# The second MLP's output products by seven products of quarters for eight, and squares of queries and keys loaded directly into SBUF

## The chip, the cores and the metric

The kernel runs on one core of one Trainium2 chip. The metric is the device time of one execution in microseconds (us). Engines are named as the profile names them: PE is the tensor engine (PEld its weight loads), DVE the vector engine, ACT the scalar engine, POOL the GpSimd engine, SP the engine that issues most DMAs.

## The reference

```python
scores = q @ k.T / sqrt(64)          # 4 batches, 8 heads, 576 positions, head size 64
scores = where(0 <= i - j < 64, scores, -1e9)
attn   = softmax(scores) @ v         # -> x, 2304 tokens x 512
x = (silu(x @ wg1) * (x @ wv1)) @ wo1          # first MLP, 512 -> 1536 -> 512
return (sigmoid(x @ wg2) * (x @ wv2)) @ wo2    # second MLP, the same sizes
```

Queries, keys and values are float32, the weights float64; the output is float32.

## The kernel before

Matrix products are done to nearly full float32 precision with three products of rounded operands: every operand is split into a high part (a copy on ACT) and a low part (a subtraction on DVE), and `TERMS` multiplies high by high, low by high and high by low. So one product of blocks is three matmul steps, and every operand costs one ACT and one DVE instruction more.

**Attention and first MLP** run interleaved. Tokens lie in five tiles of 512 or 384; the loop over tiles and twelve blocks of d_ff counts a number g up by three for each block: the gate product, the value product (`product`, L441), and the output product of the block before (`out_product`, L452). Work for later tiles hangs in tables `before`, `during` and `after`, keyed by g, and is issued on the engines' queues when the loop comes to that g. `plan_attention` places the attention of one 128-token block i there. For the blocks from `TURN` (8) on, queries and keys are turned by DVE transposes of 32x32 squares (`turn`, L231); for that they must lie in SBUF as squares. `to_squares` (L131) copies them into that form from DRAM to DRAM, and `load_qk` (L143) loads the result.

**Weights of the second MLP** are prepared meanwhile. The inputs are rounded from 64 bits (`round_a`, `round_b`: L384 to L399, two ACT and three DVE instructions for a tile of 128x512). For the gate and value weights `operands` makes the sums of quarters that a seven-product scheme needs (`sums`), splits them (`upper`, `lower`: L611, L616) into tiles called `stage`, and stores these in DRAM by POOL (`away`, L624). Stage tiles and raw weights share a ring of four buffers (`raw_p`). The output weights are only rounded, and stored whole (`store`, L406).

**The second MLP** takes three pairs of 384-token halves. In each, six units of d_ff run `strassen` twice (gate, then value): seven products instead of eight, each six matmul steps 384 wide (L775), with sums on DVE behind them (L761), and the product gate times value (L765). Then `outs` does the output products plainly: for each of twelve blocks of d_ff, six output tiles of 128 tokens by 512, three steps each (L840). Beside it DVE and ACT split the hidden values (`split_hidden`), load and split the output weights (`wo2_load`, `wo2_split`: L423, L427), and make the next pair's operands (`x_steps`: L95, L96, L704). Six banks of PSUM hold the sums until the end of the stage, where they are copied out (L860, L862) and stored (L864).

Each engine works its queue in order. A buffer of a pool is given again only when its last reader is done, and the DMA or instruction that wants it waits at the head of its queue.

Of the kernel before, what the change touches and what calls it, by code (L numbers as in the profile page):

```python
# [37 lines left out]
def attention_moe_moe(  # L38
# [86 lines left out]
    squares = {nm: dram.tile([128, HP, NT // 32, 32], FP32, name=f"{nm}s") for nm in "qk"}  # L125

    def to_squares(nm, b, s, hp, par):
        src = {"q": q, "k": k}[nm][b, 2 * hp + par, s:S]
        for a in range(2):
            r0 = 64 * par + 32 * a  # L130
            nc.sync.dma_start(  # L131
                out=squares[nm][r0:r0 + 32, hp, (b * S + s) // 32:(b + 1) * S // 32, :],
                in_=src[:, 32 * a:32 * a + 32].rearrange("(t r) d -> r t d", r=32),
            )

    def load_qk(i, pool=None):
        if i < TURN:
            nat[i, "q"] = load_tokens(q, "q", 128 * i, pool)
            nat[i, "k"] = load_tokens(k, "k", 128 * i, pool)
            return  # L140
        for nm, n in (("q", 4), ("k", 6)):
            t = nat_p.tile([128, HP, n, 32], FP32, tag=nm, name=nm)
            nc.sync.dma_start(out=t, in_=squares[nm][:, :, 4 * i + 4 - n:4 * i + 4, :])  # L143
            nat[i, nm] = t
# [210 lines left out]
    def rows(key):  # L355
# [4 lines left out]
        if wide:  # L360
            src = src.bitcast(INT32)
        if nm == "o":
            return src[fc * 128:(fc + 1) * 128, :]
# [3 lines left out]
    def load_raw(key):  # L367
        r = raw_p.tile([128, 1024 if wide else 512], INT32 if wide else FP32, tag="raw", name="raw")
        dst = r if key[1] == "o" else r.rearrange("p (c f) -> p c f", c=CC)
        nc.sync.dma_start(out=dst, in_=rows(key))  # L370
        raws[key] = r
# [31 lines left out]

    def store(key):
        kept[key] = dram.tile([128, 512], FP32, name=f"k{key[0]}{key[1]}{key[2]}")
        nc.gpsimd.dma_start(out=kept[key], in_=mids.pop(key))  # L406
# [55 lines left out]
    def finish(acc, t, n):  # L462
        for e in range(CC):
# [29 lines left out]
    def plan_attention(i, base, t, col):  # L493
# [8 lines left out]
        if base >= 2:  # L502
            at(during, base - (5 if i < TURN else 6), load_qk, i)
# [26 lines left out]
    for b in range(B):  # L530
        s = max(0, 128 * TURN - W - b * S)
        if s >= S:
            continue
        parts = [(nm, b, s, hp, par) for hp in range(HP) for par in range(2) for nm in "kq"]
        first, last = {1: (10, 24), 2: (25, 41), 3: (46, 77)}[b]
        for j, part in enumerate(parts):
            at(during, first + j * (last - first) // (len(parts) - 1), to_squares, *part)
# [45 lines left out]
    wd = {}  # L583

    def operands(u, j, nm, following):
# [34 lines left out]
        def away(k):  # L620
            if nm == "g":
                n = len(GROUPS[k])
                wd[j, k] = dram.tile([128, 2, n, 2, 256], FP32, name=f"wd{j}_{k}")
            nc.gpsimd.dma_start(out=wd[j, k][:, "gv".index(nm)], in_=stages[k][0].bitcast(FP32))  # L624
# [6 lines left out]
        at(during, u, lower, 0)  # L631
        at(during, u, round_b, keys[1])
        at(during, u, sums, 1)
        at(during, u + 1, away, 0)
# [3 lines left out]
        at(during, u + 2, lower, 1)  # L638
        at(during, u + 2, sums, 3)
        at(during, u + 3, away, 1)  # L640
        at(during, u + 3, lower, 2)
        at(during, u + 4, away, 2)
        at(during, u + 5, upper, 3)
        at(during, u + 6, lower, 3)
        at(during, u + 7, away, 3)
        if following:
            nm_, j_ = following
            at(during, u + 1, load_raw, (1, nm_, 2 * j_))
            at(during, u + 3, load_raw, (1, nm_, 2 * j_ + 1))

    for fc, g in enumerate((39, 41, 43, 46, 48, 50, 52, 57, 59, 61, 66, 68)):
        key = (1, "o", fc)
        at(during, g - 7, load_raw, key)
        at(during, g - 1, round_a, key)
        at(during, g, round_b, key)
        at(during, g + 1, store, key)
    starts = [73, 82, 91, 100, 108, 116, 124, 132, 140, 148, 156, 164]
    groups = [(nm, j) for j in range(JJ) for nm in "gv"]
    at(during, starts[0] - 9, load_raw, (1, "g", 0))
    at(during, starts[0] - 6, load_raw, (1, "g", 1))  # L660
# [154 lines left out]
    def split_hidden(fc):  # L815
        t = []
        for k in range(2):
            t.append(w_p.tile([128, 2, N2], FP32R, tag="g", name="hs"))
            split(t[k][:, 0], t[k][:, 1], hidden[fc][:, k])
        hs[fc] = t  # L820
        hidden.pop(fc)

    def wo2_load(fc):
        t = t_p.tile([128, 512], FP32, tag="t", name="tw")
        nc.sync.dma_start(out=t, in_=kept[1, "o", fc])
        mids[1, "o", fc] = t

    def wo2_split(fc):
        split_hi((1, "o", fc))
        split_lo((1, "o", fc))  # L830

    def outs(p):

        steps = x_steps(p + 1) if p + 1 < PAIRS else []
        acc = [next_bank() for _ in range(6)]
        for fc in range(FC):
            h, w = hs.pop(fc), wts.pop((1, "o", fc))
            for e in range(6):
                for n, (a, b) in enumerate(TERMS):
                    nc.tensor.matmul(  # L840
                        out=acc[e],
                        lhsT=h[e // 3][:, a, e % 3 * 128:(e % 3 + 1) * 128],
                        rhs=w[:, b],
                        start=(fc == 0 and n == 0),
                        stop=(fc == FC - 1 and n == 2),
                    )
            if fc + 2 < FC:
                split_hidden(fc + 2)
                wo2_split(fc + 2)
            if fc + 3 < FC:  # L850
                wo2_load(fc + 3)
            run_steps(steps[0:2] if fc else steps[0:1])
            steps = steps[2:] if fc else steps[1:]
            if fc >= FC - 4:
                w_ahead((p + 1) * JJ * 7 + 3 * (fc - FC + 5))
        assert not steps
        for e in range(6):
            o = t_p.tile([128, 512], FP32, tag="t", name="o")
            if e % 2:
                nc.vector.tensor_copy(o, acc[e])  # L860
            else:
                nc.scalar.activation(out=o, in_=acc[e], func=ACTF.Copy)  # L862
            r0 = p * 2 * N2 + e * 128
            nc.sync.dma_start(out=out[r0:r0 + 128, :], in_=o)  # L864
# [21 lines left out]
    with tc.manual_schedule():  # L886
# [93 lines left out]
        for p in range(PAIRS):  # L980
            for j in range(JJ):
                s = gates()
                beside = []
                if p == 0 and j == 0:
# [9 lines left out]
                    beside = [first, last_outs, lambda: run_steps(steps0[-1:])]  # L994
                strassen(p, j, 0, s, beside)
                if j == JJ - 1:
                    for fc in range(3):
                        wo2_load(fc)
                    for fc in range(2):
# [37 lines left out]
```

## Time and profile before

| | us |
|---|---|
| median of three runs (951.26 to 952.54) | 951.34 |
| the profiled execution | 953.93 |
| its span from first to last instruction | 952.2 |
| PE busy | 937.4 |
| DVE busy | 620.4 |
| ACT busy | 455.2 |

The profiled execution is 2.6 us above the median. Its span ends 1.7 us short of its own time. From 39 us to 541 us the first MLP runs, then the second in three pairs. The three output stages lie at 626.3, 762.7 and 899.1 us and are 49.0 us long each.

### The profile page before, as it was taken

The numbers are of one execution on the slowest core, as the hardware profiler recorded it, in microseconds if no ns is written. First come the engines' busy times: TensorE is split into PE (matmuls) and PEld (weight loads), VectorE is DVE, ScalarE is ACT, GpSimd is POOL, SyncE is SP. The second block draws the span as 40 slices with busy tenths as digits, with TensorE's granted clock in tenths as the row PEclk, the third lists the DMA queues.
The fourth block names the chain that finished last, engine by engine and source line by source line (L and its number), as shares of the span: only waits on it lengthen the run. The fifth ranks groups of instructions, "written<-read, shape, count | busy, mean of one in ns | idle before, by whom it ended". The sixth has DMA issues, their size and how long they took to land.

```text
span 952.2 us, 15825 instructions
## 1 busy us (share of the span) xinstructions
PE 937.4 (98%) x5699; PEld 840.1 (88%) x5699; DVE 620.4 (65%) x1407; ACT 455.2 (48%) x1010; POOL 84.6 (9%) x155
## 2 busy tenths in 40 slices
PE   7899999999999999999999999999999999999998
PEld 6688889899888888888999999988999988999986
DVE  6999985656665565654656566686466684665842
ACT  6898886655565446536344412154221443212332
POOL 3401012100200002100311000000000000000000
PEclk9999999999999999999999999999999999999999
DMA  9679887999976657755799376625868427866411
GB/s 225 190 239 277 269 244 210 307 280 287 285 232 190 198 169 258 221 193 184 242 332 387 137 267 222 246 67 182 268 252 283 152 85 229 290 233 237 139 34 66
DMA packets 183133, 209.70 MB, mean 220 GB/s; under 512 B 89488, under 2 KB 127376, under 8 KB 183056
## 3 DMA queue, kind: packets, MB, share of 16 engines
q1 hardware_dynamic: 171536, 169.38, 57.2%
q0 software_dynamic: 9792, 33.04, 9.5%
q10 hardware_dynamic: 1728, 6.29, 1.7%
q8 instruction: 45, 0.74, 0.3%
q14 instruction: 32, 0.26, 0.1%
HBM read 167.77 MB, written 46.40 MB: 225 GB/s over the span
## 4 chain that ended last, share of the span: by engine, by line
PE 93%; DMA 2%; DVE 2%; ACT 1%; issue 1%; POOL 0%; SPq 0%; DVEq 0%; ACTq 0%
PE g L441 15%; PE v L441 15%; PE a L452 15%; PE a L775 14%; PE att L775 7%; PE a L840 7%; PE att L840 3%; PE v L775 3%; PE g L775 3%; PE g L840 3%; PE v L840 3%; PE att L329 2%; PE att L249 1%; PE att L313 1%; DMA wd<-stage 1%; DVE z L268 1%
## 5 line engine op out<-in xcount | busy, mean ns | idle before, releaser
L452 PE MATMUL a<-h,wo 128*128 128x512 f32 (+1 forms) x720 | 161.4, 372 | 0.3 <-ACT z L286 0.3
L441 PE MATMUL v<-x,wv 128*128 128x512 f32 (+1 forms) x720 | 160.0, 370 | 0.0
L441 PE MATMUL g<-x,wg 128*128 128x512 f32 (+1 forms) x720 | 159.4, 370 | 0.4 <-ACT x L339 0.3
L441 PEld LDWEIGHTS g<-x,wg 128*128 128x128 f32 x720 | 130.7, 188 | 18.4 <-ACT x L339 0.6
L452 PEld LDWEIGHTS a<-h,wo 128*128 128x128 f32 x720 | 129.4, 188 | 19.3 <-issue 2.1
L441 PEld LDWEIGHTS v<-x,wv 128*128 128x128 f32 x720 | 129.9, 188 | 16.6
L775 PE MATMUL a<-xs,wop 128*128 128x384 f32 x756 | 136.2, 334 | 0.0
L775 PEld LDWEIGHTS a<-xs,wop 128*128 128x128 f32 x756 | 131.5, 188 | 0.1
L966 DVE TENSOR_TENSOR s<-s,v 128x512 f32<-128x512 f32 (+1 forms) x60 | 37.9, 632 | 80.8 <-PE v L441 69.7
L767 ACT ACTIVATE s<-s 128x384 f32<-128x384 f32 x72 | 37.9, 526 | 82.2 <-DVE s L761 82.0
L775 PE MATMUL att<-xs,wop 128*128 128x384 f32 x384 | 71.7, 334 | 0.0
L840 PE MATMUL a<-wo,hs 128*128 128x512 f32 x288 | 71.2, 389 | 0.0
L968 ACT ACTIVATE h<-s 128x512 fp32r<-128x512 f32 (+1 forms) x60 | 35.2, 586 | 75.2 <-DVE s L966 75.1
L775 PEld LDWEIGHTS att<-xs,wop 128*128 128x128 f32 x384 | 67.1, 188 | 0.1
L959 ACT ACTIVATE s<-g 128x512 f32<-128x512 f32 (+1 forms) x60 | 33.2, 553 | 67.6 <-PE g L441 66.9
L840 PEld LDWEIGHTS a<-wo,hs 128*128 128x128 f32 x288 | 54.0, 188 | 11.1
L286 ACT ACTIVATE z<-z,nm 128x128 f32<-128x128 f32 x144 | 55.8, 389 | 1.1 <-DVE nm L268 0.9
L397 DVE TENSOR_SCALAR raw<-raw 128x512 uint16<-128x512 uint16 x72 | 55.1, 765 | 1.9 <-ACT raw L384 1.9
L399 DVE CUSTOM_DVE_ANT_0 t<-raw,t 128x1024 uint16<-128x1024 uint16 x72 | 50.2, 697 | 2.5
L384 ACT ACTIVATE raw<-raw 128x512 int32<-128x512 uint32 x72 | 48.4, 672 | 6.2 <-DMA raw<-in_moe_w_out_dram 3.0
L761 DVE TENSOR_TENSOR s<-s,a 128x384 f32<-128x384 f32 x65 | 35.1, 553 | 22.6 <-PE a L775 22.1
L423 ACT ACTIVATE wo<-tw 128x512 fp32r<-128x512 f32 x36 | 22.6, 627 | 54.1 <-PE a L840 26.0
(141 smaller groups left out, 1341.1 us busy)
## 6 DMA issues: line engine op xcount, KB each, us to landing
wop<-wd SPq DMA_DIRECT2D x126, 512.0 KB, 6.0
wo<-k0o SPq DMA_DIRECT2D x48, 512.0 KB, 4.8
wd<-stage POOLq DMA_DIRECT2D x36, 512.0 KB, 5.0
raw<-in_moe_w_gate_dram SPq DMA_DIRECT2D x24, 512.0 KB, 4.7
raw<-in_moe_w_val_dram SPq DMA_DIRECT2D x24, 512.0 KB, 5.4
raw<-in_moe_w_out_dram SPq DMA_DIRECT2D x24, 512.0 KB, 5.7
tw<-k1o SPq DMA_DIRECT2D x36, 256.0 KB, 3.1
k0o<-wo ACTq DMA_DIRECT2D x12, 512.0 KB, 4.9
```

The costliest lines, as they stand in the source:

```text
L286: nc.scalar.activation(out=z[:, hp, :], in_=z[:, hp, :], func=ACTF.Exp, scale=-1.0, bias=nm[:, hp:hp + 1], accum_out=su[:, hp:hp + 1],)
L384: nc.scalar.activation(out=lower, in_=lower.bitcast(UINT32), func=ACTF.Copy, scale=2.0 ** -29)
L397: nc.vector.tensor_scalar(second, fourth, 0x8000, None, ALU.bitwise_and)
L399: nc.vector.tensor_tensor(out=t, in0=t, in1=lower, op=ALU.add)
L441: nc.tensor.matmul(out=ps[:, 0:n], lhsT=w[:, a, c, :], rhs=xt[:, b, c, 0:n], start=(j == 0), stop=(j == len(mm) - 1),)
L452: nc.tensor.matmul(out=acc[e][:, 0:n], lhsT=w[:, a, e * 128:(e + 1) * 128], rhs=h[:, b, 0:n], start=(fc == 0 and j == 0), stop=(fc == FC - ...
L761: nc.vector.tensor_tensor(out=to[out], in0=to[a], in1=ps, op=ALU.add)
L767: nc.scalar.activation(out=to[which], in_=to[which], func=ACTF.Sigmoid)
L775: nc.tensor.matmul(out=ps, lhsT=w[:, val, a, c, :], rhs=xops[op, b][:, c], start=(n == 0), stop=(n == len(mm) - 1),)
L840: nc.tensor.matmul(out=acc[e], lhsT=h[e // 3][:, a, e % 3 * 128:(e % 3 + 1) * 128], rhs=w[:, b], start=(fc == 0 and n == 0), stop=(fc == F ...
L966: nc.vector.tensor_tensor(out=s, in0=s, in1=vps[:, 0:n], op=ALU.mult)
L968: nc.scalar.activation(out=h[:, 0, 0:n], in_=s, func=ACTF.Copy)
```

## The change

Output products: the hidden values and the output weights are cut in quarters (two halves of d_ff units, two halves of tokens or columns), and seven products of sums of quarters take the place of eight, with matmul steps 256 wide. `operands` now prepares the output weights too (six more groups, and closer `starts`), `away` is issued earlier, and `outs` is new. For queries and keys the copies through DRAM go away: `load_squares` loads pieces into SBUF directly, queries by SP and keys by POOL. `turn` transposes only the block's own 128 keys; the 64 before are copied by POOL. Half of the stores of the first MLP's output move from POOL to ACT.

```diff
-    def to_squares(nm, b, s, hp, par):
...
+    def load_squares(i, nm, c, par):
+        if (i, nm) not in nat:
+            nat[i, nm] = nat_p.tile([128, HP, 4, 32], FP32, tag=nm, name=nm)
+        src, eng = {"q": (q, nc.sync), "k": (k, nc.gpsimd)}[nm]
+        for off, m, b, s in runs(128 * i, 128):
+            for a in range(2):
+                r0 = 64 * par + 32 * a
+                eng.dma_start(
+                    out=nat[i, nm][r0:r0 + 32, c, off // 32:(off + m) // 32],
+                    in_=src[b, 2 * c + par, s:s + m, 32 * a:32 * a + 32].rearrange("(t r) d -> r t d", r=32),
...
-        nc.vector.transpose(t, src)
+            nc.gpsimd.tensor_copy(t[:, :, 0:W], st[i - 1, "kt"][:, :, 128:])
+        nc.vector.transpose(t[:, :, -128:], src)
...
-                nc.gpsimd.dma_start(out=x1d[j][:, e, at_:at_ + step], in_=o[:, done:done + step])
+                (nc.gpsimd if e % 2 else nc.scalar).dma_start(out=x1d[j][:, e, at_:at_ + step], in_=o[:, done:done + step])
...
+                at(during, base - 9 + j * 6 // (4 * HP), load_squares, i, "kq"[j % 2], j // 4, j // 2 % 2)
...
-    starts = [73, 82, 91, 100, 108, 116, 124, 132, 140, 148, 156, 164]
+    starts = [39, 48, 58, 66, 75, 81, 87, 93, 100, 107, 114, 120, 126, 132, 138, 145, 155, 161]
+    groups = [("o", j) for j in range(JJ)] + [(nm, j) for j in range(JJ) for nm in "gv"]
...
+    OUT = (1, 2, 6, 7, 5, 4, 3)
+    def h_parts(op, j):
+        (e0, e1), (o0, o1) = [[hidden[2 * j + i][:, n] for n in range(2)] for i in range(2)]
+        if op == 6:
+            y = t_p.tile([128, 512], FP32, tag="t", name="y")[:, 0:N2]
+            h_minus(y, o1, e0)
+            split(*hop(op, j), y)
+            h_minus(o0, o0, y)
+        else:
+            split(*hop(op, j), {1: e0, 2: o0, 7: e1, 5: e0, 4: o0, 3: o1}[op])
...
+    def w2_ahead(upto):
...
+            nc.sync.dma_start(out=t.bitcast(FP32), in_=wdo[k][:, j:j + 2, GROUPS[k].index(op)])
...
+        for k, op in enumerate(OUT):
+            acc = [next_bank()[:, 0:256] for _ in range(3)]
+            for j in range(JJ):
+                i = (7 * p + k) * 3 + j // 2
+                h, w = hops.pop((op, j)), w2s[i][:, j % 2]
+                for e in range(3):
+                    for n, (a, b) in enumerate(TERMS):
+                        nc.tensor.matmul(out=acc[e], lhsT=h[a][:, e * 128:(e + 1) * 128], rhs=w[:, b],
...
+                if j % 2:
+                    w2s.pop(i)
+                    w2_ahead(min(i + 6, (p + 1) * 21))
+                for _ in range(2 if k == 0 and j % 3 == 1 else 1):
+                    if parts:
+                        h_parts(*parts.pop(0))
+                if k >= 2 and (k * JJ + j) % 2 == 0:
+                    run_steps(steps[0:1])
...
+            for e in range(3):
+                if op == 1:
+                    nc.scalar.activation(out=room(0)[e], in_=acc[e], func=ACTF.Copy)
+                elif op == 2:
+                    add(1, 0, acc, e)
+                    leave(1, e)
...
+                if j:
+                    beside = [lambda j=j, n=n: h_early(j - 1, n) for n in range(3)]
```

The first quarters of five of the six units (`h_early`) are made during the units before the stage. What `add` and `leave` issue are additions from PSUM on DVE and stores of 128x256.

The first output stage on PE, before (`a_...`, `g`, `v` are PSUM banks, `hs` the split hidden values, `wo` the split weights):

```order
L840 MATMUL a_6781<-wo,hs 128x512 x3
L840 MATMUL a_6782<-wo,hs 128x512 x3
L840 MATMUL a_6783<-wo,hs 128x512 x3
L840 MATMUL a_6784<-wo,hs 128x512 x3
L840 MATMUL g<-wo,hs 128x512 x3
L840 MATMUL v<-wo,hs 128x512 x3
```

and now, where the first unit of d_ff of the first and of the second of the seven products stand (`w_...` are the loaded sums of weights):

```order
L895 MATMUL a_7162<-w_7074,hs 128x256 x3
L895 MATMUL a_7163<-w_7074,hs 128x256 x3
L895 MATMUL a_7164<-w_7074,hs 128x256 x3
...
L895 MATMUL a_7254<-w_7080,hs 128x256 x3
L895 MATMUL g<-w_7080,hs 128x256 x3
L895 MATMUL v<-w_7080,hs 128x256 x3
```

Six banks for the whole stage became three banks for each of seven products, and the steps are half as wide.

On DVE the last stage's work before was a repeated pair, splits of hidden values (L96) and of weights (L427), behind the last product gate times value (L765):

```order
L761 TENSOR_TENSOR hid<-hid,a_9342 128x384
L765 TENSOR_TENSOR hid<-hid,s 128x384
L96 TENSOR_TENSOR hs<-hid,hs 128x384 x2
L427 TENSOR_TENSOR wo<-tw,wo 128x512
L96 TENSOR_TENSOR hs<-hid,hs 128x384 x2
```

Now, at the start of the first output stage (L757 is the product gate times value, L824 a difference of hidden quarters, `y` a scratch tile):

```order
L757 TENSOR_TENSOR hid<-hid,s 128x384
L96 TENSOR_TENSOR hs<-hid,hs 128x384
L824 TENSOR_TENSOR hid<-hid 128x384 x2
L96 TENSOR_TENSOR hs<-hid,hs 128x384 x6
L824 TENSOR_TENSOR y<-hid 128x384
L96 TENSOR_TENSOR hs<-y,hs 128x384
L824 TENSOR_TENSOR hid<-hid,y 128x384
...
L96 TENSOR_TENSOR hs<-hid,hs 128x384 x2
L878 TENSOR_TENSOR o<-o,a_7254 128x256
L878 TENSOR_TENSOR o<-o,g 128x256
L878 TENSOR_TENSOR o<-o,v 128x256
```

The group of three with `y` stands six times, and all of it stands ahead of the additions (L878) that free the second product's banks.

On POOL, in the third tile, the stores of stage tiles stood alone before:

```order
L624 DMA wd_0_3139<-stage 128x1024
L624 DMA wd_1_3203<-stage 128x1024
L624 DMA wd_2_3240<-stage 128x1024
L624 DMA wd_3_3344<-stage 128x512
```

and now there are loads of key squares (L136) between them:

```order
L622 DMA wdo_2055<-stage 128x1024
L226 COPY kt<-kt 128x4x64
L622 DMA wdo_2128<-stage 128x1024
L136 DMA k<-in_k_dram 32x2x32 x8
L622 DMA wdo_2156<-stage 128x1024
L136 DMA k<-in_k_dram 32x2x32 x16
L622 DMA wdo_2270<-stage 128x512
```

This is the block with the most pieces, 32; the other nine have 16.

## Rows read from the trace of the kernel before

**Rows 1.** The page's head: span, then busy time and instructions of each engine.

```profile
span 952.2 us, 15825 instructions
PE 937.4 (98%) x5699; PEld 840.1 (88%) x5699; DVE 620.4 (65%) x1407; ACT 455.2 (48%) x1010; POOL 84.6 (9%) x155
```

**Rows 2.** Busy time by window: first MLP, two output stages, seven-product units.

```profile
core 0: us, PE busy (x) PEld busy (x) DVE busy (x) ACT busy (x) POOL busy (x), PEclk, DMA share, GB/s
356.00:462.00 106.00, 106.00 (x613) 86.79 (x612) 60.90 (x142) 56.31 (x125) 15.18 (x26) 1.00 0.66 220
626.30:675.30 49.00, 49.00 (x218) 40.58 (x217) 31.67 (x61) 19.98 (x42) 0.00 (x0) 1.00 0.51 163
...
899.10:948.10 49.00, 49.00 (x217) 40.37 (x216) 20.77 (x39) 13.99 (x28) 0.00 (x0) 1.00 0.09 29
840.00:890.00 50.00, 50.00 (x290) 50.00 (x290) 32.62 (x64) 10.06 (x20) 0.00 (x0) 1.00 0.73 256
```

**Rows 3.** Chain that ended last: start us, us, engine, tile, line, count.

```profile
471.82 7.61 DMA wd<-stage
480.59 2.38 PE g L441 x12
...
543.29 4.16 PE a L775 x24
...
626.49 2.76 PE a L840 x12
630.61 2.72 PE a L840 x12
```

**Rows 4.** PE, then its weight loads, in order of time; brackets: idle before.

```profile
98.18 0.60 PE L313 MATMUL att<-ident,z 128*128 128x128 f32 x4
...
480.59 1.01 PEld L441 LDWEIGHTS g<-x,wg 128*128 128x128 f32 x6 [0.51 <-ACT s L959]
```

**Rows 5.** DVE in order of time, first output stage and behind it; brackets: idle before.

```profile
629.60 1.02 DVE L96 TENSOR_TENSOR hs<-hid,hs 128x384 fp32r<-128x384 f32 x2
...
636.59 0.56 DVE L704 TENSOR_TENSOR rx<-rx 128x384 f32<-128x384 f32 x1
637.74 0.56 DVE L96 TENSOR_TENSOR xs<-rx,xs 128x384 fp32r<-128x384 f32 x1 [0.59 <-ACT xs L95]
638.22 0.55 DVE L704 TENSOR_TENSOR rx<-rx 128x384 f32<-128x384 f32 x1
...
690.51 0.55 DVE L761 TENSOR_TENSOR hid<-hid,a 128x384 f32<-128x384 f32 x1
691.09 0.56 DVE L765 TENSOR_TENSOR hid<-hid,s 128x384 f32<-128x384 f32 x1
```

**Rows 6.** Instruction groups by form: count | busy us, mean ns | idle before, releaser.

```profile
L96 DVE TENSOR_TENSOR hs<-hid,hs 128x384 fp32r<-128x384 f32 x72 | 36.8, 552 | 3.0 <-ACT hs L95 3.0
L95 ACT ACTIVATE hs<-hid 128x384 fp32r<-128x384 f32 x72 | 33.3, 510 | 0.0
L624 POOL DMA_DIRECT2D wd<-stage x48 | 28.8, 601 | 215.9 <-DVE stage L616 172.3 <-issue 25.2 <-DVE su L302 10.8
L427 DVE TENSOR_TENSOR wo<-tw,wo 128x512 fp32r<-128x512 f32 x36 | 24.8, 689 | 29.8 <-ACT wo L423 29.8
L313 PE MATMUL att<-ident,z 128*128 128x128 f32 x112 | 16.1, 272 | 0.0
L601 DVE TENSOR_TENSOR t<-n,t 128x256 f32<-128x256 f32 x12 | 5.0, 420 | 0.0
```

**Rows 7.** DMA issues: queue, count, KB each, median us to landing.

```profile
wop<-wd SPq DMA_DIRECT2D x126, 512.0 KB, 6.0
```

**Rows 8.** Waits: engine and line, for whom: us in total, times, longest.

```profile
ACT stage L611 <- DMA wd<-stage: 12.4, 5, 5.7
```

**Rows 9.** DVE in order of time: its last instruction.

```profile
948.30 0.69 DVE L860 COPY o<-a 128x512 f32<-128x512 f32 x1 [0.67 <-PE a L840]
```

**Rows 10.** Seven-product steps into one bank: count, ns min/median/max, first and last start us.

```profile
L775 PE MATMUL g<-xs,wop x186: 334/334/334, 536.9 to 891.6; 128*128 128x384 f32 x186
```

More of the change, by code (lines that the diff above doesn't have):

```diff
@@ L361, in rows @@
             src = src.bitcast(INT32)
+        if nm == "o" and m == 1:
+            w = DM // 2 * width
+            pair = src[fc // 2 * 256:(fc // 2 + 1) * 256, fc % 2 * w:(fc % 2 + 1) * w]
+            return pair.rearrange("(s p) f -> p s f", p=128)
         if nm == "o":
@@ L813, in gates @@
         return s
[L815 to L830, printed above, removed]
+    OUT = (1, 2, 6, 7, 5, 4, 3)
@@ new lines, in attention_moe_moe, with hop, h_minus @@
+    hops = {}
+    w2s = {}
+    next_w2 = [0]
+    def hop(op, j):
+        if op == 1 and j < 5:
+            at_ = ((p_p, "z0"), (p_p, "z1")), ((p_p, "pt0"), (qt_p, "qt"))
+            tiles = at_[j] if j < 2 else ((t_p, "t"),) * 2
+            t = [pool.tile([128, 512], FP32R, tag=tag, name="hs")[:, 0:N2] for pool, tag in tiles]
+        else:
+            t = w_p.tile([128, 2, N2], FP32R, tag="g", name="hs")
+            t = [t[:, 0], t[:, 1]]
+        hops[op, j] = t
+        return t
+    def h_minus(out, a, b):
+        nc.vector.tensor_tensor(out=out, in0=a, in1=b, op=ALU.subtract)
@@ new lines, in h_parts, with h_early @@
+    def h_parts(op, j):
[5 more added lines that the diff above has]
+            h_minus(o0, o0, y)
+        else:
+            split(*hop(op, j), {1: e0, 2: o0, 7: e1, 5: e0, 4: o0, 3: o1}[op])
+    def h_early(j, step):
+        e, o1 = hidden[2 * j], hidden[2 * j + 1][:, 1]
+        if step == 0:
+            h_parts(1, j)
+        elif step == 1:
+            h_minus(e[:, 0], e[:, 1], e[:, 0])
+        else:
+            h_minus(e[:, 1], o1, e[:, 1])
@@ new lines, in w2_ahead @@
+    def w2_ahead(upto):
+        while next_w2[0] < min(upto, PAIRS * 21):
+            i = next_w2[0]
+            op, j = OUT[i // 3 % 7], i % 3 * 2
+            k = [op in group for group in GROUPS].index(True)
+            n = i // 21 * 16 + i % 21 - 5
+            pool, tag = (w_p, "g") if i % 21 < 5 else (wo_p, "o") if n % 5 < 3 else (h_p, "h")
+            t = pool.tile([128, 2, 2, 256], FP32R, tag=tag, name="w2")
+            nc.sync.dma_start(out=t.bitcast(FP32), in_=wdo[k][:, j:j + 2, GROUPS[k].index(op)])
+            w2s[i] = t
+            next_w2[0] += 1
@@ L832, in outs @@
     def outs(p):
         steps = x_steps(p + 1) if p + 1 < PAIRS else []
-        acc = [next_bank() for _ in range(6)]
-        for fc in range(FC):
[L837 to L864, printed above, removed]
+        parts = [(op, j) for op in OUT[1:] for j in range(JJ)]
+        rows = [[], [], [], []]
+        made = {}
@@ new lines, in room @@
+        def room(i):
+            if len(rows[i]) == 3:
+                return rows[i]
+            places = {0: (0, 0, 1), 1: (2, 2, 3), 2: (1, 6, 6), 3: (4, 4, 5)}[i]
+            tags = ((p_p, "z0"), (p_p, "pt0"), (h_p, "s"), (h_p, "s"), (kt_p, "v"), (kt_p, "v"), (p_p, "z1"))
+            for n in places:
+                if n not in made:
+                    pool, tag = tags[n]
+                    made[n] = [pool.tile([128, 2, 256], FP32, tag=tag, name="o"), 0]
+                rows[i].append(made[n][0][:, made[n][1]])
+                made[n][1] += 1
+            return rows[i]
@@ L866, in bank_of @@
+        run_steps(steps)
+        for fc in range(FC):
+            hidden.pop(fc)
     def bank_of(tag):
```

116 lines of the change are left out of this document (61 added, 55 removed).

## Prediction

> **What bounds the kernel now.** I read the head of the page first, then busy time by window, then the chain of waits, and then the rows of single instructions. PE is busy 937.4 of 952.2 us [rows 1], and the chain that ended last is a chain of PE groups at one fixed pace [rows 3]. Twelve steps 512 wide take 2.72 us, 0.2267 each; twenty-four steps 384 wide take 4.16 us, 0.1733 each. The difference, 0.0533 us for 128 columns, is 2.4 columns per ns, which is the upper of the two clock levels; the granted clock is 1.00 in all these windows [rows 2]. What is left over is 0.0133 us for every step, whatever its width: 0.2267 − 512/2400. An output stage of 216 steps is then 48.97 us, and the stage measures 49.0 [rows 2]. So the output stage has no gap in it, and every us that leaves PE there comes off the time, as long as DVE keeps up. DVE is busy 31.7 of the 49.0 us in the first stage and 20.8 in the last, which prepares no next pair [rows 2].
>
> **The output products.** Before, a stage is 12 blocks x 6 tiles x 3 = 216 steps of 512. After, it is 7 products x 6 units x 3 tiles x 3 = 378 steps of 256. Columns fall to exactly 7/8 (96,768 for 110,592), 5.76 us less at 2.4 columns per ns; but 162 more steps pay 0.0133 us each, 2.16 us. A step 256 wide is not in this trace. By the straight line through the two widths it takes 256/2400 + 0.0133 = 0.120 us, and a stage 45.4 us: 3.6 us less, 10.9 for the three stages. From below, the bound is what a weight load allows, since each step loads 128x128 new weights: four transposes 128 wide, each with such a load, took 0.60 us in all, and a single one is 0.272 in the mean of their group, so one follows another by about 0.11, (0.60 − 0.272)/3 [rows 4, 6]. At 0.11 a stage would be 41.6. From above, the bound is the 384-wide step, 0.1733. I take 0.120, because both measured widths lie on one line and the load does not reach up to it.
>
> One rule of the Trainium skill gives another figure. TensorE: Matmul & The Clock Gate, section Back-to-back issue gap, puts a warm isolated step at N/2.4 ns plus 2.5 ns. For 512 columns that would be 216 ns, and the trace shows 227 [rows 3], so I keep the measured 13.3 ns of overhead. By that rule a 256-wide step would be 109 ns by estimate and the PE work of a stage 41.3 us.
>
> **DVE beside it.** Removed from a stage are 24 splits of hidden values, 12 splits of weights (0.69 us) and three copies out. Now there are 37 splits (0.51 us, 36.8/72), 14 differences of the same size (0.55) and 21 additions 256 wide (0.42, taken from the SBUF sums of that width) [rows 6]: 18.9 + 7.7 + 8.8 = 35.4 us. The first two stages add the next pair's operands, 31.7 − 20.8 = 10.9 us [rows 2], 46.3 in all, while PE needs 45.4. So DVE is as full as PE there, and the deadlines decide. A part of that sum (the last additions and operands, some 4 us) may run over into the next unit, where DVE is busy 32.6 of 50 us [rows 2].
>
> Two places are close. The first is the third product, whose operand `y` goes DVE, ACT, DVE. This pattern stands in the trace with rx in place of y: from 636.59 to 638.22, with 0.59 us idle for ACT [rows 5]. One such group with its second difference is 2.1 us. DVE is done with the last gate-times-value 1.8 us after PE leaves a unit (it ends at 691.65, and PE at 675.3 + 84 x 0.1733 = 689.9 [rows 2, 3, 5]). Then come 1.5 us for the sixth unit's first quarters and 2.8 us for six splits, since a second independent one follows by 0.47 (1.02 us for two [rows 5]). So `y` starts at 6.1 us, and the sixth split of it is ready at 6.1 + 5 x 2.1 + 1.7 = 18.3 us. PE asks for it at 2 x 6.48 + 5 x 1.08 = 18.4. The second place is the last product, whose sixth quarter I find ready at about 44.1 to 44.5 us, by adding up the same durations in the order shown; PE asks for it at 44.3. I take 0.5 us of stall for each of the first two stages and 0.2 for the last, 1.2 in all. The bounds are 0 and about 9, which is DVE's 46.3 plus 3.6 of idling for ACT, against 45.4, in two stages.
>
> **Loads in the stage.** Each sum of weights is 512 KB and serves 18 steps, 2.16 us, so 243 GB/s. The seven-product units already load at 256 GB/s, with 512 KB landing in 6.0 us, and PE has no gap [rows 2, 3, 7]. Ten of the 21 loads are issued before the stage, and each later one five tiles (10.8 us) ahead. I cost it at nothing; without that lead it would be up to 4 us a stage. ACT, at 20 of 49 us [rows 2], has room for its splits and for the issue of half the first MLP's stores.
>
> **The end.** The last matmul is followed now by a copy of 0.69 us [rows 9], then a store of 256 KB, and the span ends 3.2 us after that copy. Afterwards an addition of 0.42 us and a store half as large close it. I take 0.5 us off (bounds 0 and 1.5).
>
> **First MLP.** Preparing six more groups adds 4 sums and a 256-wide split at 0.42 and three splits at 0.69 on DVE, 4.2 us each, 25 us in all, and some 14 us on ACT. DVE is busy there 57% (60.9 of 106 us [rows 2]) and goes up to some 65%; PE runs without gaps [rows 3]. Transposes of keys get a third smaller. The copies through DRAM (96 DMAs, and 20 loads) become 176 pieces on SP and 176 on POOL. At about 0.6 us to issue one on POOL [rows 6] the latter are 106 us, beside 85 us now over the whole run [rows 1]. Behind them on POOL stand the stores of stage tiles, and for these stores the ring of four buffers waits, for that ACT, for that the gate activation, and for that PE. That chain exists already: the store at 471.82 took 7.6 us and PE resumed only at 480.59, after ACT had waited [rows 3, 8]. It cost PE about 0.5 us once (the idle time in brackets ahead of the weight loads at 480.59 [rows 4]). With 18 groups for 12, six or seven steps of g apart in the middle, I put it at 1.5 us (below, 0: the earlier stores and the DRAM traffic saved undo it; above, 1 us for each of 18 groups).
>
> **Sum.** −10.9 + 1.2 − 0.5 + 1.5 = −8.7 us. The profiled execution, 953.9, would become 945.2; it lies 2.6 above the median of the runs, so the median goes from 951.3 to 942.6.
>
> **Rivals.**
> DVE becomes the bound of the output stages. For it: 46.3 us of work against 45.4, and in-order idling for ACT that a count does not show. Against it: the work of the next pair can slip, and the last stage has no such work. With most of the 9 us, it comes to about 948 (945.5 to 951). Chance 0.17.
>
> Slower: POOL's key pieces delay the stores of stage tiles. Up to 32 pieces stand around two stores of one group, 19 us at 0.6 us, while three steps of g are about 8.2 us (3 x 2.72, a group of twelve 512-wide steps). ACT then waits for the ring, its activations come late, and PE stalls. For it: the one stall of this kind in the trace [rows 3, 4, 8]. Against it: the same waits add up to 12.4 us on ACT and cost PE only about 0.5, so there are some us of cover; most blocks have 16 pieces, and a piece is small. It decides from 0.57 us per group (10.2/18); at 1 us for each it is 951.3 − 10.2 + 18 = 959, where 10.2 is the gain without the 1.5 us of the first MLP. Chance 0.12.
>
> Slower too: a 256-wide step does not follow the line. At 0.130 us the gain is gone (49.0/378); at the upper bound, 0.173, a stage is 65.5 us and the whole 1001. Against it: weight loads follow each other at 0.11 [rows 4]. Chance 0.05.
>
> Faster still: the 0.0133 us of each step hides behind something in narrow steps, and the step comes at the pace of the loads, 0.11 us. The last stage then gains 7.4 us and the two others are held by DVE's 46.3, 2.7 each: 951.3 − 12.8 − 0.5 + 1.5 = 939.5. For it: the 128-wide transposes show no such overhead beyond their loads [rows 4]. Against it: the overhead is the same at both wider widths. Chance 0.08. (The formula of the Trainium skill cited above leads close to this time.)
>
> The new loads come late (the change then does not do what it says in full). For it: 243 GB/s plus next-pair operands and weights at the end of a stage. Against it: the sustained 256 GB/s. With up to 2 us a stage, 947 to 949. Chance 0.04.
>
> **How the numbers follow.** The forecast holds 0.54 with its own range of 939 to 946. The range of 8 in 10 reaches from 938 to 951, leaving out most of the two slower rivals and the end of the fast one. A measurement of this kernel tells 0.2%, about 1.9 us, from no change. Faster by more than that: 0.54, 0.14 of the DVE rival, 0.08, and 0.02 of the late loads: 0.78. Slower: 0.16, nearly all of the POOL and the step rivals. Same: the rest, 0.06.
>
> **What would show it.** Right, if the output stages take 45 to 46.5 us, with 256-wide groups of three following each other by 0.36 us; if PE idles at most 1 us a stage, and then for DVE's split of `y` or of the last quarters; if DVE's busy time in the first two stages is above 44 us; and if the gate banks' first product of the second MLP starts within 2 us of 536.9 [rows 10]. Wrong, if groups of three are 0.39 us apart or more, if PE waits over 2 us in a stage for DVE or a load, or if the second MLP starts later than 540.

## The result and the profile after

The median goes from 951.39 us (951.26 to 952.54, with the kernel before run again on the same chip) to 942.87 us (941.83 to 942.93). The ratio is 0.9905, interval 0.9888 to 0.9922, so 9.0 us less (7.4 to 10.7); the two medians lie 8.5 us apart. The forecast was 942.6.

The head of the page after answers to [rows 1]:

```profile
span 941.0 us, 17596 instructions
PE 928.2 (99%) x6185; PEld 856.7 (91%) x6185; DVE 693.4 (74%) x1599; ACT 469.6 (50%) x1052; POOL 211.5 (22%) x368
```

PE still bounds the kernel. DVE has 73 us more to do and POOL 127 us more, and neither has become the bound. The same windows as in [rows 2], for the first MLP, the three output stages, and a seven-product unit:

```profile
core 0: us, PE busy (x) PEld busy (x) DVE busy (x) ACT busy (x) POOL busy (x), PEclk, DMA share, GB/s
356.00:462.00 106.00, 106.00 (x614) 86.88 (x613) 69.33 (x157) 62.12 (x136) 34.33 (x55) 1.00 0.73 237
625.80:671.40 45.60, 45.59 (x379) 45.38 (x379) 41.30 (x91) 20.99 (x50) 3.24 (x6) 1.00 0.66 229
758.80:804.40 45.60, 45.59 (x379) 45.38 (x378) 41.30 (x91) 20.99 (x50) 3.23 (x6) 1.00 0.67 228
891.80:937.40 45.60, 45.59 (x379) 45.36 (x378) 32.98 (x75) 16.20 (x37) 4.83 (x9) 1.00 0.49 154
840.00:890.00 50.00, 50.00 (x290) 50.00 (x289) 35.35 (x70) 11.88 (x25) 0.00 (x0) 1.00 0.78 273
```

Each output stage takes 45.6 us for the 49.0 of [rows 2]. The granted clock is 1.00 in all of them. In the chain of waits (start us, us, what), groups of three new steps follow each other by 0.36 us, so a step takes 0.120 us:

```profile
652.14 0.36 PE g L895 x3
652.50 0.36 PE v L895 x3
652.86 0.36 PE att L895 x3
```

What the output steps waited for (line 895 of the changed kernel; us, times) is one operand, once a stage:

```profile
its engine sat idle before it (us, times) until:
  DVE hs L96: 0.6, 3
```

DVE's rows of the first stage, in order of time, show where:

```profile
642.59 0.55 DVE L824 TENSOR_TENSOR y<-hid 128x384 f32<-128x384 f32 x1
643.78 0.56 DVE L96 TENSOR_TENSOR hs<-y,hs 128x384 fp32r<-128x384 f32 x1 [0.64 <-ACT hs L95]
```

PE's weight loads, in order of time, show the wait:

```profile
644.39 0.65 PEld L895 LDWEIGHTS att<-w,hs 128*128 128x128 f32 x5 [0.21 <-DVE hs L96]
```

DVE subtracts, idles 0.64 us while ACT rounds the difference, and splits it at 643.78. PE asks for that split 18.4 us after the stage's start at 625.8, and gets it 0.2 us late: this is the sixth `y` of the third product. From it on, 0.21 us is lost.

The end, as in [rows 9], is now a short addition:

```profile
937.63 0.42 DVE L878 TENSOR_TENSOR o<-o,att 128x256 f32<-128x256 f32 x1
```

The chain's stretch with the 7.61 us store and the gap at 480.59 [rows 3] is unbroken now, groups of twelve every 2.08 us:

```profile
478.27 2.08 PE a L449 x12
480.35 2.08 PE g L438 x12
482.43 2.08 PE v L438 x12
```

The first seven-product step, which was at 536.9 in [rows 10], marks the end of the first MLP (duration ns min/median/max, first and last start us):

```profile
L767 PE MATMUL g<-xs,wop x186: 334/334/334, 536.3 to 886.4; 128*128 128x384 f32 x186
```

Weights of the seven-product units take longer to land than in [rows 7], and no PE row waits for them:

```profile
wop<-wd SPq DMA_DIRECT2D x126, 512.0 KB, 7.0
w<-wdo SPq DMA_DIRECT2D x63, 512.0 KB, 6.1
```

The profiled execution of before lies 2.5 us above its median and that of after at its median, so I compare first MLPs by medians: a kernel's median, less 1.8 us outside the span, less its time from the first seven-product step to the end in its own profile (415.3 us before, 404.7 after). By that the second MLP starts at 534.3 before and at 536.4 after, 2.1 us later; in the profiled runs it was 536.9 and 536.3. Such a figure is good to about 1 us: that time came out at 404.7 to 405.8 us in the seven profiled kernels with the same second MLP as after, and nearly all of the difference is the store that closes the kernel.

### The profile page after: what moved, and what is told of

Read it like the earlier page. It is cut to its first block, busy times and chain, and to the rows that moved or that the text cites. A ratio compares the mean times of both kernels' runs of the same rounds, so it can differ in the third digit from the quotient of the medians.

```text
span 941.0 us, 17596 instructions
## 1 busy us (share of the span) xinstructions
PE 928.2 (99%) x6185; PEld 856.7 (91%) x6185; DVE 693.4 (74%) x1599; ACT 469.6 (50%) x1052; POOL 211.5 (22%) x368
## 4 chain that ended last, share of the span: by engine, by line
PE 94%; DVE 2%; ACT 2%; DMA 1%; issue 0%; POOL 0%; ACTq 0%; DVEq 0%
PE g L438 15%; PE a L449 15%; PE v L438 15%; PE a L767 14%; PE a L895 8%; PE att L767 7%; PE v L767 4%; PE g L767 3%; PE att L895 3%; PE g L895 2%; PE v L895 2%; PE att L325 2%; PE att L245 2%; PE att L309 1%; DMA x1d<-o 1%; DVE z L264 1%
## 5 line engine op out<-in xcount | busy, mean ns | idle before, releaser
L438 PEld LDWEIGHTS g<-x,wg 128*128 128x128 f32 x720 | 130.7, 188 | 18.4 <-ACT x L335 0.6
L767 PE MATMUL a<-xs,wop 128*128 128x384 f32 x738 | 133.1, 334 | 0.0
L767 PEld LDWEIGHTS a<-xs,wop 128*128 128x128 f32 x738 | 128.4, 188 | 0.0
L136 POOL DMA_DIRECT2D k<-in_k_dram x176 | 101.4, 583 | 38.9 <-PE att L195 23.3
L884 POOL DMA_DIRECT2D out_dram<-o x33 | 17.7, 541 | 372.9 <-DVE o L878 372.2
L895 PE MATMUL a<-w,hs 128*128 128x256 f32 x594 | 81.1, 283 | 0.0
L895 PEld LDWEIGHTS a<-w,hs 128*128 128x128 f32 x594 | 75.6, 191 | 0.2 <-DVE hs L96 0.2
L767 PE MATMUL att<-xs,wop 128*128 128x384 f32 x396 | 74.0, 334 | 0.0
L622 POOL DMA_DIRECT2D wd<-stage x48 | 33.3, 695 | 135.8 <-DVE stage L608 125.5
L96 DVE TENSOR_TENSOR hs<-hid,hs 128x384 fp32r<-128x384 f32 x108 | 55.0, 552 | 7.3 <-ACT hs L95 7.3
L95 ACT ACTIVATE hs<-hid 128x384 fp32r<-128x384 f32 x108 | 49.4, 512 | 15.9 <-DVE hid L757 11.4
```

What stands on the lines that cost most here:

```text
L95: nc.scalar.activation(out=dst_hi, in_=src, func=ACTF.Copy)
L96: nc.vector.tensor_tensor(out=dst_lo, in0=src, in1=dst_hi.bitcast(FP32), op=ALU.subtract)
L136: eng.dma_start(out=nat[i, nm][r0:r0 + 32, c, off // 32:(off + m) // 32], in_=src[b, 2 * c + par, s:s + m, 32 * a:32 * a + 32].rearrange(" ...
L438: nc.tensor.matmul(out=ps[:, 0:n], lhsT=w[:, a, c, :], rhs=xt[:, b, c, 0:n], start=(j == 0), stop=(j == len(mm) - 1),)
L622: nc.gpsimd.dma_start(out=dst, in_=stages[k][0].bitcast(FP32))
L767: nc.tensor.matmul(out=ps, lhsT=w[:, val, a, c, :], rhs=xops[op, b][:, c], start=(n == 0), stop=(n == len(mm) - 1),)
```

## The experiments

Each row of the table is a kernel of its own. A median in brackets is a single profiled run; the starts and stages are those of the profiled runs.

| Kernel | Median us (profiled run) | Ratio to before (interval) | Second MLP starts at | Output stages |
|---|---|---|---|---|
| before | 951.39 | 1 | 536.9 | 49.0, 49.0, 48.9 |
| after | 942.87 | 0.9905 (0.9888–0.9922) | 536.3 | 45.6 ×3 |
| output products alone | 948.92 | 0.9952 (0.9935–0.9968) | 540.7 | 45.6 ×3 |
| direct squares alone | 952.50 | 0.9999 (0.999–1.0008) | 534.8 | 49.0, 49.0, 48.9 |
| output products, copies on SP and POOL | 942.21 | 0.9895 (0.988–0.991) | 535.7 | 45.6 ×3 |
| output products, copies on POOL | 942.37 | 0.9897 (0.9881–0.9914) | 535.5 | 45.6 ×3 |
| after, with the copies too | 968.70 | 1.0171 (1.015–1.0193) | 559.7 | 45.6 ×3 |
| after, all pieces on POOL | 983.02 | 1.0321 (1.0301–1.0341) | 576.5 | 45.6 ×3 |
| after, all pieces on SP | 975.63 | 1.0239 (1.0206–1.0272) | 567.5 | 45.6 ×3 |
| after, 12 more DVE operations a stage | 950.17 | 0.9978 (0.9967–0.999) | 536.0 | 49.0, 49.0, 46.6 |
| after, short lead of loads | 970.26 | 1.0188 (1.0165–1.0211) | 538.9 | 59.6, 59.0, 45.6 |
| after, steps 128 wide | (1057.96) | – | 535.4 | 84.4 ×3 |
| after, differences on POOL | (945.51) | – | 537.5 | 45.7, 45.5, 45.5 |
| before, once more | (956.09) | – | 539.0 | 49.0, 49.0, 48.9 |

### How far the first MLP scatters: the kernel before, once more

> The kernel before, unchanged, profiled once more: its first profiled execution took 953.9 us, 2.6 above the median of its runs. If the 2.6 us belong to a place of the program, the span is again near 952 and all stages are as long; if they were of that execution alone, the span is near 949.7, and the comparison by stages shows in which stage the first execution lost them. The three output stages are 49.0 us each in either case.

The code is that of before, and its output stages are 49.00 us again. The first MLP ended 2.1 us later (539.0); PE lost 2.4 us in one gap at 267.8 us that the first profile does not have. Five profiled programs with the same first MLP as after began the second at 535.4 to 538.9. One profile therefore tells nothing below 3 us of the first MLP, and the stages repeat to 0.1 us.

### The two halves of the change

Output products alone: the new stages, with the squares still copied through DRAM by 96 DMAs on SP's queue and loaded from there.

```diff
+    squares = {nm: dram.tile([128, HP, NT // 32, 32], FP32, name=f"{nm}s") for nm in "qk"}
+            nc.sync.dma_start(out=squares[nm][...], in_=src[...])
...
-            for j in range(4 * HP):
-                at(during, base - 9 + j * 6 // (4 * HP), load_squares, i, "kq"[j % 2], j // 4, j // 2 % 2)
```

> The new output products and weight groups as in the changed kernel, but squares of queries and keys go through DRAM as before. Theory (PE steps set the gain; the squares are off PE's path): output stages 45.6 us each, three of them 10 us below before; time within 2 us of the changed kernel's 942.9. Rival (the direct squares bring a part of the gain by relieving the DRAM and DVE): 945 or more, with the first MLP longer by 2 us or more.

Direct squares alone: the 352 pieces, with the old output stages.

```diff
-    squares = {nm: dram.tile([128, HP, NT // 32, 32], FP32, name=f"{nm}s") for nm in "qk"}
+    def load_squares(i, nm, c, par):
...
+        src, eng = {"q": (q, nc.sync), "k": (k, nc.gpsimd)}[nm]
```

> The kernel before with the direct squares alone; output products plain. Theory: output stages 49.0 us each, second MLP starts at 536.9 plus or minus 1 us, time 951.3 plus or minus 2. Rival (the 176 key pieces on POOL hold up stage tiles, and the extra weight groups hide that in the changed kernel): slower than 953. Other rival (they bring a part of the gain): below 949.

The new stages alone save 4.6 us by the ratio (3.4 between the medians), with the stages at 45.63 us as in after. The first MLP takes back the rest: by medians it ends 6.2 us later than before, by the ratio 5.0. The squares alone are worth nothing (interval −0.1 to +0.1%). Yet both together give 9.0, so what the squares bring shows only beside the six more groups of weights. What they bring was open at this point: less traffic, or less on SP's queue. The stores that the change moves to ACT stand in every kernel with the new products, and no run has them alone.

### Is it the traffic? The copies beside the pieces

```diff
+    squares = {nm: dram.tile([128, HP, NT // 32, 32], FP32, name=f"{nm}s") for nm in "qk"}
+            nc.sync.dma_start(out=squares[nm][...], in_=src[...])
+            at(during, first + j * (last - first) // (len(parts) - 1), to_squares, *part)
```

The copies are made in their old places, and nothing reads them.

> The changed kernel, with the 96 copies of squares from DRAM to DRAM issued as before beside it; nobody reads what they write. It tells why the new output products alone (with squares through DRAM) started the second MLP at 540.7 us, 4.4 later than with direct squares. Theory (the 16 DMA engines are full from 150 to 275 us, and the copies' traffic makes loads and stage tiles late): the DMA share there goes up to 0.95 or more, PE loses 3 to 6 us in the first MLP, second MLP starts at 539 to 542, time 945.5 to 948.5. Rival (it is the order of loads and transposes of the old way, six squares of keys a block, and not the traffic): start at 536 to 537.5, time within 1.5 us of 942.9.

968.7 us, far from either figure. The edit was a poor one: it doubled the traffic of the squares, but SP then issued the copies ahead of its 176 pieces as well, and the late pieces show: the wait of DVE for a query tile (us, times, longest) runs behind a transfer of SP's queue.

```profile
DVE qt L238 <- DMA ks<-in_k_dram: 10.5, 1, 10.5
```

It settles neither theory.

### Is it SP's queue? The same copies from other queues

Two kernels, both output products alone, all traffic kept; only the queue that issues the copies differs.

```diff
-            nc.sync.dma_start(
+            eng.dma_start(                     # queries nc.sync, keys nc.gpsimd
```

> The new output products with the copies of queries and keys through DRAM kept, but the 96 copies shared out as the pieces are in the changed kernel: queries on SP's queue, keys on POOL's. With all copies on SP the profiled second MLP began at 540.7 us and the median was 0.9952 of before. Theory A (those 4 us are SP's queue, in which the copies stand ahead of weight loads): the second MLP begins at 536 to 538 and the ratio is 0.991 to 0.993. Theory B (they are the traffic of writing and reading the squares once more, together with six more groups' tiles): the queue changes nothing, the start stays at 539.5 to 542 and the ratio at 0.994 to 0.997.

```diff
-            nc.sync.dma_start(
+            nc.gpsimd.dma_start(
```

> The same, with all 96 copies on POOL's queue and none on SP's. Theory A (SP's queue): start at 536 to 538 and ratio 0.990 to 0.993, unless the copies delay the stores of stage tiles on POOL; then ACT waits over 15 us in all for the ring of stage tiles. Theory B (traffic): start at 539.5 to 542, ratio 0.994 to 0.997, and ACT's waits for that ring stay under 15 us.

Both come out on A's side, a little beyond its ranges: 942.21 and 942.37 us, starts 535.7 and 535.5, as good as the changed kernel. Busy time in three stretches of the first MLP (columns as in [rows 2]; the first two overlap by 5 us), with all copies on SP:

```profile
150.00:180.00 30.00, 27.84 (x206) 25.91 (x205) 18.28 (x52) 16.87 (x39) 4.97 (x8) 1.00 0.83 244
175.00:205.00 30.00, 28.77 (x219) 27.71 (x218) 19.15 (x57) 18.67 (x45) 3.33 (x5) 1.00 1.01 305
245.00:275.00 30.00, 28.53 (x185) 23.37 (x184) 22.02 (x54) 19.08 (x43) 5.99 (x10) 1.00 1.03 311
```

The same stretches with the copies split:

```profile
150.00:180.00 30.00, 29.63 (x218) 27.82 (x217) 20.31 (x60) 18.48 (x46) 8.24 (x12) 1.00 0.84 263
175.00:205.00 30.00, 30.00 (x227) 29.22 (x226) 19.89 (x59) 21.80 (x59) 9.29 (x13) 1.00 1.00 300
245.00:275.00 30.00, 30.00 (x193) 24.69 (x192) 21.48 (x53) 20.19 (x50) 6.08 (x9) 1.00 0.95 301
```

The DMA engines are nearly as full (the last two columns), and PE's waits between 150 and 280 us fall from 4.9 us in four places to 0.4 in one. The kernel before, with all copies on SP too, loses 1.7 us between 175 and 205. SP's own waits between 140 and 280 us fit this. With all copies on SP (us in total, times, longest):

```profile
SPq L375 <- DMA wdo<-stage: 3.2, 2, 1.9
```

With the copies split:

```profile
SPq L376 <- DMA wdo<-stage: 48.7, 8, 8.6
```

This is the line that loads raw weights, waiting for its buffer. With the copies split, SP reaches it early and has 48.7 us to spare; with all of them on SP it arrives when the buffer is long free, so the load itself is late. A wait of SP for this buffer is slack in these kernels. The 96 copies take a median of about 0.6 us each on SP (ns min/median/max, first and last start us):

```profile
L131 SPq DMA_DIRECT2D ks<-in_k_dram x48: 551/608/2499, 71.0 to 258.2; - x48
L131 SPq DMA_DIRECT2D qs<-in_q_dram x48: 550/636/2925, 72.3 to 261.2; - x48
```

Behind them loads arrive late. Waits of ACT and DVE between 140 and 280 us, with all copies on SP:

```profile
ACT raw L389 <- DMA raw<-in_moe_w_out_dram: 6.1, 2, 3.6
DVE kt L231 <- DMA k<-ks: 3.0, 1, 3.0
```

The Trainium skill (DMA: Bandwidth & Descriptors, section Issuing engines are not separate DMA queues) holds that DMAs of all issuing engines share the same 16 DMA engines and that spreading them saves only the issuer's time, usually small beside the transfer. The shared engines agree with the nearly equal traffic above, and an issue of 0.6 us is small beside the median of 4.8 us that a copy takes to land. What the saved time is worth is another matter here: 48 copies of about 0.6 us moved off SP bring 6.7 us (948.92 to 942.21; as ratios, 0.9952 to 0.9895, 5.4 us). What is not separated is whether SP loses the time in issuing or in the order of transfers behind it.

### The slower rival at a higher dose: all pieces on one queue

```diff
-        src, eng = {"q": (q, nc.sync), "k": (k, nc.gpsimd)}[nm]
+        src, eng = {"q": (q, nc.gpsimd), "k": (k, nc.gpsimd)}[nm]
```

> The changed kernel, but the query pieces are issued by POOL too: 352 pieces there for 176, some 200 us of issuing between 100 and 440 us. Theory of cover (POOL has slack, the ring of stage tiles has some us of cover): PE keeps its pace in the first MLP, time within 2 us of 942.9. Rival (POOL's pieces delay stage tiles, ACT and so PE): stores of stage tiles are issued late, the second MLP starts 5 us or more later than 536.3, time 948 or more.

```diff
-        src, eng = {"q": (q, nc.sync), "k": (k, nc.gpsimd)}[nm]
+        src, eng = {"q": (q, nc.sync), "k": (k, nc.sync)}[nm]
```

> The changed kernel with the key pieces issued by SP too, 352 there and none on POOL. After the run with all pieces on POOL (983 us, stage tiles stored late), it tells whether the 176 pieces on POOL still cost something in the changed kernel. If POOL's queue costs some us: stage tiles are stored earlier, ACT waits less than 9 us for them between 140 and 360 us, time 939 to 941.5. If it costs nothing and SP has room: 942 to 944. If SP's queue is as narrow as POOL's (0.5 us a piece, behind loads that wait): raw weights and reloads come late, 950 or more.

On POOL alone they cost 983.0 us, 40 us more than after. The chain is the rival's: ACT waits for the ring of stage tiles and PE for ACT. ACT's waits for the ring with all pieces on POOL (us, times, longest):

```profile
ACT stage L603 <- DMA wdo<-stage: 44.9, 10, 14.9
```

PE in order of time there, with its longest gap in brackets:

```profile
317.20 0.47 PE L325 MATMUL att<-pt,v 128*64 128x64 f32 x2 [10.81 <-ACT pt L315]
```

The stretch around it, as a window:

```profile
300.00:340.00 40.00, 23.75 (x144) 18.87 (x144) 14.01 (x33) 10.92 (x19) 33.00 (x60) 0.79 0.46 145
```

ACT's wait for the same ring in the changed kernel:

```profile
ACT stage L603 <- DMA wdo<-stage: 8.9, 4, 2.9
```

POOL is busy 33 of 40 us, and the granted clock falls to a mean of 0.79 while PE waits, which makes the loss larger. In after, the wait exists (8.9 us of ACT), and PE's gaps between 140 and 400 us are 1.0 us in all. SP alone is not better: 975.6 us, and there ACT waits for raw gate weights behind the pieces (16.4 us in three places, 9.2 the longest). Neither queue has room for 352 pieces; each has room for 176.

### Is DVE as full as the forecast said?

```diff
+                if k >= 1 and j % 3 == 0:
+                    h_minus(extra, hidden[j][:, 0], hidden[j][:, 1])
```

Twelve subtractions a stage, whose result nothing reads. Each spans 0.55 us, but they follow each other by 0.47, so they are 5.6 us; DVE's busy time in the last stage rises by 5.5, from 33.0 to 38.5.

> The changed kernel with 12 more differences 384 wide on DVE in every output stage, from the second product on (two for each product, into a scratch tile that nothing reads): 5.6 us of DVE work a stage at 0.47. Theory (DVE is as full as PE in the first two stages, with deadlines met by some tenths of a us): these two stages grow from 45.6 to 49 to 51 us, the last by about 1 us (its third product only), and the whole by 8 to 12 us. Rival (PE alone bounds the stage, DVE has room): each stage grows by less than 0.5 us, the whole by less than 2.

The first two stages grow by 3.34 us each, the last by 0.95. So DVE has about 2.3 us of room there and some 4.6 in the last, and that although it still idles 8 of 46.6 us in the last: the deadline of a single split decides, not the sum. What is added beyond the room comes out on PE. Its steps and weight loads together waited, over all stages (us, times), for DVE's splits and for the additions that free banks:

```profile
  DVE hs L96: 6.1, 15
  DVE o L878: 3.9, 4
```

### Do the loads need their lead?

```diff
-                    w2_ahead(min(i + 6, (p + 1) * 21))
+                    w2_ahead(min(i + 3, (p + 1) * 21))
```

> The changed kernel, but in the output stages each of the last eleven loads of weight sums is issued when the tile two before it is used up, for five before: a lead of one tile, 2.16 us, where a load takes about 6 to land. Theory (the loads are hidden by their lead): from the eighth tile on PE waits for each load, two tiles take 6.5 to 8.3 us for 4.3, a stage grows by 10 to 22 us and the whole by 30 to 65. Rival (loads land in about 2 us when few are under way): growth under 5 us in all.

The first two stages grow by 14.0 and 13.3 us, the last by nothing. PE waits for loads, over all stages (us, times, longest):

```profile
PE a L895 <- DMA w<-wdo: 13.0, 6, 5.2
PE att L895 <- DMA w<-wdo: 2.1, 1, 2.1
```

and in the windows at the end of the first stage the granted clock is lower, beside full DMA engines:

```profile
660.00:670.00 10.00, 7.91 (x54) 7.74 (x53) 9.93 (x25) 5.42 (x13) 1.62 (x3) 0.83 0.97 320
670.00:687.00 17.00, 9.29 (x60) 8.67 (x59) 5.65 (x13) 2.58 (x6) 1.60 (x3) 0.80 0.96 326
```

PE is busy 49.8 and 50.3 us in these two stages for 45.6, as its steps are longer at the lower clock, and idles for the rest of the growth. Here the next pair's operands and weights are loaded too. The last stage has no such traffic, and even the short lead is enough.

### What a narrower step costs

```diff
+                        for part in (slice(0, 128), slice(128, 256)):
...
+                                out=acc[e][:, part],
+                                rhs=w[:, b, part],
```

Each product step becomes two of 128 columns, each with its own weight load.

> The changed kernel with every 256-wide step of the output stages cut into two 128 wide, each with its own load of the same weights: 756 steps a stage. If a step is 13.3 ns plus columns at 2.4 per ns at any width: 66.7 ns each, a stage 50.4 us. If a load of 128x128 weights is the floor at 108 ns: a stage 81.6 us. If narrow steps pay for float32 operands some other way: longer than that.

A stage takes 84.37 us, 0.1116 us for each of 756 steps. By the line it would be 0.0667, so a floor sets the pace here. The first stage as a window has PE and PEld busy throughout:

```profile
625.00:709.00 84.00, 84.00 (x755) 84.00 (x754) 45.28 (x96) 23.04 (x50) 5.06 (x10) 1.00 0.51 164
```

A 256-wide step at 0.120 therefore lies just above this floor. The weight load is its likely cause; no run has 128-wide steps without loads of their own, so that is not shown. By the Trainium skill (TensorE: Matmul & The Clock Gate, section LDWEIGHTS (loading the stationary operand)) a load of 128 columns takes 128/1.2, by estimate 107 ns; 111.6 measured is near it. The gap of N/2.4 + 2.5 ns in the section Back-to-back issue gap of the same page of the Trainium skill, by estimate 109 for 256 columns, falls under the measured floor, and 120 was measured.

### Can the last stall be had? Differences on POOL

```diff
-            nc.vector.tensor_tensor(out=ts[out, c], in0=ts[a, c], in1=ts[b, c], op=ALU.subtract)
+            eng = nc.gpsimd if p else nc.vector
+            eng.tensor_tensor(out=ts[out, c], in0=ts[a, c], in1=ts[b, c], op=ALU.subtract)
...
-            h_minus(o0, o0, y)
+            nc.gpsimd.tensor_tensor(out=o0, in0=o0, in1=y, op=ALU.subtract)
```

> The changed kernel with the second difference of each y group, and the differences of the next pair's operands, on POOL instead of DVE: 2.8 us less DVE work in each stage and 4 us less in the first two. Theory (the little that PE still loses in the stages is DVE's lateness): stages 45.4 us in place of 45.6, first and third stage without the wait in the third product; the whole 0.5 to 1 us less, too little to be told by the time alone. Rival (what PE loses is something else, or POOL is slower than the deadlines): stages of 45.6 or longer.

The second difference of each `y` group is off DVE in all three stages. The last two fall to 45.51 us, the first is 45.71. The second pair's units take 89.05 us for 87.36, and PE waits there for its loads (1.2 us in two places). No gain: what was to be had is 0.1 us a stage.

## Why the prediction was right

**Output stages.** The step is 0.120 us, as the line through two widths gave it. Three stages went from 146.9 to 136.9 us, 10.0 less; the terms −10.9 and +1.2 make −9.7. The stall is 45.63 − 378 × 0.120 = 0.27 us a stage, 0.8 in all, and the third product's sixth `y` is where one was forecast (asked for at 18.4 us, forecast 18.4). The last quarters brought none that the rows show.

**DVE.** One of the signs named was wrong: DVE's busy time in the first two stages is 41.3 us and not above 44. Some of the work ran past the stage's end, as the text said it might: the additions after 671.40, in DVE's order of time, are still from this stage.

```profile
673.21 0.75 DVE L878 TENSOR_TENSOR o<-o,a 128x256 f32<-128x256 f32 x2
673.88 0.42 DVE L878 TENSOR_TENSOR o<-o,g 128x256 f32<-128x256 f32 x1
```

With what follows until 674.3 it is at most 44.2 us, and the last stage has at most 33.4 with its closing addition. So the counts, 46.3 and 35.4, were too high: the sum took nearly the full span of each instruction, and spans of successive ones overlap (two additions of 0.42 us take 0.75 above). "As full as PE" was therefore too strong: added operations found 2.3 us of room. That the deadlines decide held.

**Loads.** They cost nothing, as forecast. The lead was mis-told: load i + 5 is issued when tile i is done, so four tiles and 8.6 us, not 10.8. With 8.6 against a landing of 6.1 us it is enough; with 2.2 us it costs 27 us, more than the "up to 4 us a stage" that I gave for a missing lead. That figure left out next-pair traffic and the clock.

**The end.** −0.57 us (4.29 to 3.72 from the start of the last step to the span's end), forecast −0.5. The same end took 3.7 to 4.7 us in the profiles of the other kernels with the new products 256 wide, and the old one 4.3 to 4.6, so a single pair of profiles does not show half a us.

**First MLP.** +2.1 us by medians (1.6 by the ratio), forecast +1.5. The 2.1 is what the medians leave when the other terms are taken off, so the sum −10.0 − 0.6 + 2.1 = −8.5 closes by its making. Two other kernels with the same first MLP, the one with more DVE operations and the one with the short lead, give 1.3 and 1.7 in the same way. The size was right, the reasoning was not, and that this term came out is luck. I expected POOL's pieces to cost it, and counted the removed copies as a possible small gain. The runs show the pieces alone cost nothing (0.9999), six more groups cost 5.0 to 6.2 us as long as the copies stand on SP, and 0.6 to 0.7 by medians when they do not. So the first MLP waited in places for what SP's queue brought late, which I never put in the sum: I had looked at who waits for POOL, and not at how much SP has to spare. The forecast came right because the change takes the 96 copies off SP in the same stroke and puts the key squares on POOL. The 176 query pieces stand on SP, and yet it has slack again. Its wait with a raw load between 140 and 280 us in the changed kernel (us, times, longest):

```profile
SPq L371 <- DMA wdo<-stage: 34.2, 5, 10.6
```

For the output products alone the same sum, without pieces on POOL, would have given 951.3 − 10.2 = 941.1, and 948.9 was measured. Whether POOL's pieces, beside the six groups, cost the 1 us or so by which the first MLP of after lies above the 0.6 to 0.7 stays open.

**Rivals.** The step at the loads' pace of 0.11 us is excluded, since it was 0.120. DVE holds up PE only with more than some 2.3 us of added work a stage. The chain over POOL is real, as all pieces on POOL show, and has its cover at the dose of this change.

## What to carry to other kernels

Time of a narrower matmul step came from a straight line through two wider ones (0.120 us forecast and measured), down to a floor, here 0.112 us. When an edit adds transfers, look at how long the queue that issues them waits for free buffers: that time was its slack here (48.7 us where loads came in time, 3.2 where they came late). A queue that hardly waits for them is a suspect, and the same transfers on another queue are the test. Two edits that look unrelated may share a queue, so measure each one alone before crediting either.

## What was not expected

Who issues a copy mattered more than that it is made: 96 copies through DRAM, with their reads, cost nothing measurable when half or all of them stood on POOL (942.2 and 942.4 us, against 942.9 with the direct loads), while the DMA engines stood at shares of 0.88 to 1.00 between 175 and 275 us. The direct loads are thus not needed for this gain; the three kernels cannot be told apart.
